# Placing the gate buffers of an attention and feed-forward kernel 128 bytes further on in SBUF

## The chip, the cores and the metric

The kernel runs on one NeuronCore of a Trainium2 chip. The metric is the device time of one execution in microseconds (us), the median over several runs. PE is TensorE, the matrix engine; PEld is its weight load, which overlaps its matmuls; DVE, ACT and POOL are VectorE, ScalarE and GpSimd; SP issues the DMAs. SBUF is the on-chip memory with 128 partitions, and an address here always means the byte within each partition at which a buffer begins. PSUM is the memory into which PE writes.

## What is computed

A chunked attention with memory tokens, and behind it a feed-forward layer with a piecewise quadratic gate:

```python
# attention: 4 batches, 8 heads, 768 tokens, head_dim 64; chunks of 32 queries,
# each sees 8 memory keys, 16 keys to the left, its own 32, and 8 to the right
for c in range(nc):
    ...
    scores = scale * np.matmul(q_c, k_full.transpose(0, 1, 3, 2))
    scores = scores - np.max(scores, axis=-1, keepdims=True)
    a = np.exp(scores)
    a = a / (np.sum(a, axis=-1, keepdims=True) + 1e-09)
    out[:, :, c_start:c_end] = np.matmul(a, v_full)
# feed-forward: 3072 tokens, 512 -> 2048 -> 512
h = x @ w_in
g = np.where(pos, h, np.where(neg, 0.0, (h + beta) ** 2 / (4.0 * beta)))   # beta 1, pos: h >= 1, neg: h <= -1
return (g @ w_out).astype(np.float32)
```

## The kernel before

**Tiling.** The 3072 tokens are six blocks of 512. In each block the attention output x (512 features as four slices of 128, times 512 tokens) is made in two halves and kept as two fp32r tiles, a high part `xth` and a remainder `xtl`. The feed-forward layer goes over 16 slices of 128 hidden features (`fc`). One step is one block and one slice, so there are 96 steps.

**A step on PE** has two groups of 12 matmuls.

- `pe_hidden` (line 406) makes the hidden values of the slice in a PSUM bank `ps_h`: four matmuls of the high weights with `xth`, four of the low weights with `xth`, four of the high weights with `xtl`. The stationary operand, the one that a weight load brings in, is a 128x128 piece of a weight tile `wr`; the moving operand is 512 tokens of x.
- `pe_out` (line 441), two steps later (`LAG`), multiplies the gated values with the slice of the second weight matrix into four PSUM banks `ps_o`: eight matmuls with `gh`, the high part of the gate, and four with `gl`, its remainder. Here the gate is the stationary operand (`gh[:, ts]`, 128 of its 512 columns, so 512 bytes per partition), and the moving operand is 512 columns of a weight tile `wr`.

Each matmul has a weight load of its own, and the load of the next matmul runs beside the present one.

**Between the groups** `gating` (line 415) has ACT read `ps_h` into `gw` and `gt` and square `gw`; `gate_sum` (line 425) has DVE combine them into `gw`; `gate_high` (line 430) has ACT round `gw` to `gh`; `gate_low` (line 436) has DVE write `gl` as the difference. So `gw`, `gt`, `gh` and `gl` are the gates' buffers: two each of `gw` and `gt`, three each of `gh` and `gl`, 2,048 bytes each in a partition.

**Order.** The program is written out in full, with no loop at run time, and each engine keeps the order in which it is written. The first two blocks follow a table (`FIRST`, lines 32 to 50) that interleaves DMA loads, decoding of the weights on ACT and DVE (`decode`, line 148), attention and steps; in it some steps are split into halves of 256 tokens (`early_step`, line 452). From step 32 on, the loop at line 573 puts attention for later blocks between the steps.

**Where buffers lie.** Four pools take SBUF from low addresses to high: `const` (weights), `xpool` (x), `apool` (attention, `f`, output), `gpool` (the gates). The compiled program gives these addresses:

| buffers | first address | spacing | address mod 512 |
|---|---|---|---|
| weights `w`, `wr`, 16 tiles | 1,664 | 8,192 | 128 |
| `xth`, `xtl`, two each | 132,736 | 8,192 | 128 |
| `pr`, `pt` | 177,792 | 4,096 | 128 |
| `f` (and `ob`), two | 194,560 | 4,096 | 0 |
| `gw`, `gt`, `gh`, `gl` | 202,752 | 2,048 | 0 |

The slices that PE reads are 512 bytes apart in the weights (as stationary operand) and in the gates, and 2,048 bytes apart in x and in the weights (as moving operand), so each slice has the remainder of its buffer.

Of the kernel before, what the change touches and what calls it, by code (L numbers as in the profile page):

```python
# [8 lines left out]
F32 = mybir.dt.float32  # L9
# [7 lines left out]
P = 128  # L17
# [51 lines left out]
def attn_ffn_kernel(ctx: ExitStack, tc: tile.TileContext, first_qk, first_v, qk, vw, w, out):  # L69
# [18 lines left out]
    gpool = ctx.enter_context(tc.tile_pool(name="gpool", bufs=2))  # L88
# [447 lines left out]
    early += [(load, blk, half) for blk, half in ((1, 1), (2, 0), (2, 1), (3, 0)) for load in (load_qk, load_v)]  # L536
    early = iter(early)

    warm = gpool.tile([P, DM], BF16, name="warm", tag="gw")
    dve.memset(warm, 0.0)  # L540
    keep_warm(8)
# [162 lines left out]
```

## Time and profile before

| | |
|---|---|
| time, median of 3 runs | 608.13 us (608.02 to 608.14) |
| span of the profiled execution, first to last instruction | 606.4 us |
| PE busy, instructions | 591.0 us (97%), 5496 |
| weight loads busy, instructions | 483.7 us (80%), 5496 |
| DVE busy | 325.6 us (54%) |
| ACT busy | 281.2 us (46%) |
| mean DMA rate | 91 GB/s |

For the profiled execution only its span is given; the 1.7 us between it and the median of the runs lie outside its first and last instruction. In the profile's lists "L63" is a helper that records every operation, so the groups are told apart by the names of their tiles: `ps_o<-wr,gh` is a matmul that reads `wr` and `gh` and writes `ps_o`. The time of a matmul in these lists is that of one alone, from its start to its modelled end; neighbours overlap, so the pace of PE is the distance from one start to the next.

### The profile page before, as it was taken

What the parts mean: (1) busy time and instruction counts of PE and PEld (TensorE: products, weight loads), DVE (VectorE), ACT (ScalarE), POOL (GpSimd) and SP (SyncE); (2) the same over time, 40 slices, a digit from 0 to 9 for tenths busy, and PEclk for the clock granted to TensorE, in tenths of its full rate; (3) what the DMA queues carried; (4) which work ended last, traced back from release to release, by engine and by line L of the source; (5) the groups of instructions that cost most, each with busy time, mean ns of one, the idle gap of its engine ahead of it and who ended that gap; (6) DMA issues with size and microseconds to landing.
All of it is one profiled execution on the core that took longest, in us unless ns stands there. A gap on an engine that the chain in (4) does not pass through costs nothing.

```text
span 606.4 us, 12265 instructions
## 1 busy us (share of the span) xinstructions
PE 591.0 (97%) x5496; PEld 483.7 (80%) x5496; DVE 325.6 (54%) x466; ACT 281.2 (46%) x503; POOL 0.7 (0%) x6
## 2 busy tenths in 40 slices
PE   5889999999999999999999999999999999999996
PEld 2888888888888888888888888888888888888885
DVE  5999999987483224736424734623553632322222
ACT  2689764544444434344434434434433343533342
POOL 0000000000000000000000000000000000000000
PEclk8699999999999999999999999999999999999999
DMA  8999200433131004012201213101310000100001
GB/s 353 423 418 420 124 1 1 175 110 137 31 145 70 1 0 175 30 42 105 70 1 73 103 70 106 70 1 54 121 70 2 1 2 0 70 0 1 0 1 69
DMA packets 9845, 55.31 MB, mean 91 GB/s; under 512 B 1089, under 2 KB 1089, under 8 KB 5185
## 3 DMA queue, kind: packets, MB, share of 16 engines
q1 hardware_dynamic: 9792, 54.53, 23.2%
q8 instruction: 43, 0.70, 0.5%
q14 instruction: 10, 0.07, 0.0%
HBM read 48.23 MB, written 6.29 MB: 90 GB/s over the span
## 4 chain that ended last, share of the span: by engine, by line
PE 94%; DVE 3%; ACT 1%; DMA 1%; issue 0%; DVEq 0%; ACTq 0%
PE ps_o L63 44%; PE ps_h L63 44%; PE ps_x L63 3%; PE ps_s L63 3%; DVE f L63 1%; DMA qk<-in_first_qk_dram 1%; DVE pr L63 1%; DVE mx L63 0%; DVE den L63 0%; ACT w L63 0%; ACT gw L63 0%; DVE wr L63 0%; DVE xtl L63 0%; ACT pr L63 0%; ACT wr L63 0%
## 5 line engine op out<-in xcount | busy, mean ns | idle before, releaser
L63 PE MATMUL ps_o<-wr,gh 128*128 128x512 f32 x768 | 199.5, 396 | 0.0
L63 PE MATMUL ps_h<-xth,wr 128*128 128x512 f32 (+1 forms) x832 | 197.3, 379 | 0.0
L63 PEld LDWEIGHTS ps_h<-xth,wr 128*128 128x128 f32 x832 | 148.7, 189 | 31.9 <-DVE wr L63 0.5
L63 PEld LDWEIGHTS ps_o<-wr,gh 128*128 128x128 f32 x768 | 143.7, 188 | 32.5
L63 DVE SCALAR_TENSOR_TENSOR gw<-gw,gt 128x512 f32<-128x512 f32 (+1 forms) x104 | 67.2, 648 | 170.0 <-ACT gw L63 169.5
L63 ACT ACTIVATE gw<-ps_h 128x512 f32<-128x512 f32 (+1 forms) x104 | 58.7, 564 | 167.8 <-PE ps_h L63 167.7
L63 PE MATMUL ps_o<-wr,gl 128*128 128x512 f32 x384 | 109.0, 394 | 0.0
L63 PE MATMUL ps_h<-xtl,wr 128*128 128x512 f32 (+1 forms) x416 | 105.2, 375 | 0.0
L63 DVE TENSOR_TENSOR gl<-gw,gh 128x512 fp32r<-128x512 f32 (+1 forms) x104 | 67.4, 649 | 67.4 <-ACT gh L63 67.3
L63 ACT CAST gh<-gw 128x512 fp32r<-128x512 f32 (+1 forms) x104 | 61.1, 590 | 68.7 <-DVE gw L63 68.7
L63 PEld LDWEIGHTS ps_h<-xtl,wr 128*128 128x128 f32 x416 | 75.3, 190 | 14.1
L63 PEld LDWEIGHTS ps_o<-wr,gl 128*128 128x128 f32 x384 | 72.5, 189 | 17.2
L63 ACT ACTIVATE gw<-gw 128x512 f32<-128x512 f32 (+1 forms) x104 | 62.5, 601 | 0.0
L63 ACT ACTIVATE gt<-ps_h 128x512 f32<-128x512 f32 (+1 forms) x104 | 58.2, 559 | 0.0
L63 DVE STREAM_TRANSPOSE pt<-pr 32x512 f32<-32x512 f32 (+1 forms) x60 | 41.2, 698 | 1.3
L63 DVE SCALAR_TENSOR_TENSOR f<-w,f 128x1024 uint32<-128x1024 uint32 x32 | 38.9, 1220 | 0.4
L63 PEld LDWEIGHTS ps_x<-pt,v 64*64 64x64 f32 x1536 | 25.2, 142 | 5.5 <-issue 3.5
L63 ACT ACTIVATE pr<-pr 128x1024 f32<-128x1024 f32 (+1 forms) x14 | 13.1, 937 | 35.5 <-DVE pr L63 35.4
L63 PE MATMUL ps_x<-pt,v 64*64 64x32 f32 x1536 | 26.7, 226 | 1.6 <-ACT pt L63 1.6
L63 ACT CAST xth<-ps_x 128x512 fp32r<-128x512 f32 x24 | 13.1, 590 | 21.6 <-PE ps_x L63 21.5
L63 PEld LDWEIGHTS ps_s<-qk 64*32 64x32 f32 x1536 | 16.7, 110 | 6.4 <-issue 3.2
L63 ACT CAST wr<-f 128x1024 fp32r<-128x1024 f32 x16 | 16.8, 1050 | 9.3 <-DVE f L63 9.3
(27 smaller groups left out, 182.1 us busy)
## 6 DMA issues: line engine op xcount, KB each, us to landing
w<-in_w_dram SPq DMA_DIRECT2D x16, 1024.0 KB, 19.8
qk<-in_qk_dram SPq DMA_DIRECT2D x10, 1536.0 KB, 6.7
v<-in_vw_dram SPq DMA_DIRECT2D x10, 1024.0 KB, 5.1
out_dram<-ob SPq DMA_DIRECT2D x24, 256.0 KB, 2.0
qk<-in_first_qk_dram SPq DMA_DIRECT2D x4, 768.0 KB, 8.8
v<-in_first_v_dram SPq DMA_DIRECT2D x4, 512.0 KB, 12.8
```

What stands on the lines that cost most here:

```text
L63: return self.tc.keep_in_program_order(getattr(self.engine, name)(*args, **kwargs))
```

## The change

One line is added ahead of the first tile of `gpool`. It takes a tile of 32 fp32 values, 128 bytes in each partition, that nothing reads or writes.

```diff
     early = iter(early)
 
+    gpool.tile([P, 32], F32, name="offset", bufs=1)
     warm = gpool.tile([P, DM], BF16, name="warm", tag="gw")
     dve.memset(warm, 0.0)
     keep_warm(8)
```

In the compiled program the gates' buffers (and `warm`, a bf16 tile that shares the first `gw` buffer and feeds eight matmuls at the start) begin at 202,880 in place of 202,752, and each of them lies 128 bytes further on; their address mod 512 is 128 in place of 0. No other buffer moves. Every engine has the same instructions with the same shapes in the same order as before; only the running numbers in the names of tiles and the line numbers behind line 538 differ by one.

## The prediction

> **What bounds the kernel now.** I read the page first: the busy shares, the clock and the chain that ended last.
>
> ```profile
> PE 591.0 (97%) x5496; PEld 483.7 (80%) x5496; DVE 325.6 (54%) x466; ACT 281.2 (46%) x503; POOL 0.7 (0%) x6
> ...
> PEclk8699999999999999999999999999999999999999
> ...
> PE 94%; DVE 3%; ACT 1%; DMA 1%; issue 0%; DVEq 0%; ACTq 0%
> ```
>
> PE is the bound, at full granted clock (9 in the row PEclk) after the first slices, and waits for almost nothing. Its time is therefore the number of matmuls times their pace. The groups with their shapes kept apart give the number:
>
> ```profile
> L63 PE MATMUL ps_o<-wr,gh 128*128 128x512 f32 x768 | 199.5, 396 | 0.0
> L63 PE MATMUL ps_h<-xth,wr 128*128 128x512 f32 x704 | 178.3, 395 | 0.0
> L63 PEld LDWEIGHTS ps_h<-xth,wr 128*128 128x128 f32 x832 | 148.7, 189 | 31.9 <-DVE wr L63 0.5 <-issue 0.2
> L63 PEld LDWEIGHTS ps_o<-wr,gh 128*128 128x128 f32 x768 | 143.7, 188 | 32.5
> ...
> L63 PE MATMUL ps_h<-xtl,wr 128*128 128x512 f32 x352 | 94.7, 391 | 0.0
> ```
>
> With half as many for `gl` that is 1152 matmuls of `ps_o` and 1056 of `ps_h` at 512 columns. Read alone, a matmul or a load takes the same time in both groups (395 and 396, 189 and 188 ns). The pace does not show here; it shows in the starts. Here is the timeline of PE over one step late in the run, when no attention work is left:
>
> ```profile
> 562.70 2.01 PE L63 MATMUL ps_h<-xth,wr 128*128 128x512 f32 x8
> 564.54 1.08 PE L63 MATMUL ps_h<-xtl,wr 128*128 128x512 f32 x4
> 565.45 2.03 PE L63 MATMUL ps_o<-wr,gh 128*128 128x512 f32 x8
> 567.32 1.09 PE L63 MATMUL ps_o<-wr,gl 128*128 128x512 f32 x4
> 568.25 0.40 PE L63 MATMUL ps_h<-xth,wr 128*128 128x512 f32 x1
> ```
>
> The step takes 568.25 - 562.70 = 5.55 us. `ps_o` has 2.80 us of it, 233 ns per matmul. `ps_h` has 2.75, but not evenly: the eight with `xth` run at 1.84 / 8 = 230 ns, the four with `xtl` at 0.91 / 4 = 227.5. The same twelve `ps_h` matmuls can do better, as the timeline shows at a place where they follow a different piece of work (a half step of `ps_o` after matmuls of 256 columns):
>
> ```profile
> 148.11 1.98 PE L63 MATMUL ps_h<-xth,wr 128*128 128x512 f32 x8
> 149.92 1.08 PE L63 MATMUL ps_h<-xtl,wr 128*128 128x512 f32 x4
> 150.83 0.40 PE L63 MATMUL ps_o<-wr,gh 128*128 128x512 f32 x1
> ```
>
> That is 2.72 us for twelve, 226.7 ns each, with `xth` at 226 as well. So `ps_h` has a settled pace of 226.7 ns and usually starts behind `ps_o` at a worse one that lasts for up to eight matmuls. Whether `ps_o` ever settles is seen at the end of the run, where three steps' groups of it stand in a row:
>
> ```profile
> 593.22 2.03 PE L63 MATMUL ps_o<-wr,gh 128*128 128x512 f32 x8
> 595.09 1.08 PE L63 MATMUL ps_o<-wr,gl 128*128 128x512 f32 x4
> 596.01 2.02 PE L63 MATMUL ps_o<-wr,gh 128*128 128x512 f32 x8
> 597.87 1.10 PE L63 MATMUL ps_o<-wr,gl 128*128 128x512 f32 x4
> 598.80 0.62 PE L63 MATMUL ps_o<-wr,gh 128*128 128x512 f32 x2
> 599.26 0.39 PE L63 MATMUL ps_o<-wr,gl 128*128 128x512 f32 x1
> 599.49 0.64 PE L63 MATMUL ps_o<-wr,gh 128*128 128x512 f32 x2
> 599.97 0.40 PE L63 MATMUL ps_o<-wr,gl 128*128 128x512 f32 x1
> ```
>
> It does not: 593.22 to 598.80 is 5.58 us for 24, 232.5 ns each, and the last four of them (597.87 to 598.80) still have 232.5. In this last stretch the other engines are nearly idle, as their timelines say:
>
> ```profile
> 596.44 0.69 DVE L63 TENSOR_TENSOR gl<-gw,gh 128x512 fp32r<-128x512 f32 x1 [0.69 <-ACT gh L63]
> ...
> 600.40 0.69 DVE L63 COPY ob<-ps_o 128x512 f32<-128x512 f32 x1 [3.27 <-PE ps_o L63]
> ...
> 601.12 0.59 ACT L63 COPY ob<-ps_o 128x512 f32<-128x512 f32 x1 [4.72 <-DVE ob L63]
> ```
>
> From 597.13 to 600.40 neither DVE nor ACT runs an instruction, and `ps_o` is as slow as ever. So contention with DVE or ACT is not what costs the 6 ns.
>
> **The change part by part.** It removes, adds and reorders no instruction, adds no wait, and moves no DMA. All that is new is where the gates lie: at 128 mod 512, as weights and x do.
>
> *ACT and DVE on the gates.* Rows of the same size whose buffer (`pr`) already lies at 128 mod 512 bound this:
>
> ```profile
> L63 DVE TENSOR_TENSOR gl<-gw,gh 128x512 fp32r<-128x512 f32 x88 | 60.8, 691 | 66.4 <-ACT gh L63 66.4
> ...
> L63 ACT ACTIVATE gw<-gw 128x512 f32<-128x512 f32 x88 | 55.7, 634 | 0.0
> ...
> L63 DVE TENSOR_TENSOR pr<-pr,rin 128x512 f32<-128x512 f32 x4 | 2.8, 692 | 0.1
> ...
> L63 ACT ACTIVATE pr<-pr 128x512 f32<-128x512 f32 x4 | 2.5, 624 | 8.1 <-DVE pr L63 8.1
> ```
>
> 692 against 691 and 624 against 634 ns: I take zero. The cover is that a gate is used two steps, about 11 us, after its `ps_h`; only in the first 205 us is there little of it.
>
> *The weight loads of gates.* This is the term. What differs between a load during `ps_h` and one during `ps_o` is the buffer it reads: `wr` at 128 mod 512, as the moving operand, or a gate at 0 mod 512, which is 384 away from it. The other differences are excluded by rows above. Output banks and the repeated moving operand: at the end the order is by output, so that one bank is written three times running with the moving operand alternating, and the five matmuls from 598.80 to 599.97 (1.17 us, 234 ns each) are no faster. Waits: most of these loads wait for nothing. So I expect `ps_o` to run at the settled pace of `ps_h`, and `ps_h` to lose its slow start, since it would follow a settled group. A group of `ps_o` then goes from 2.80 to 2.72 us (0.08 less), one of `ps_h` from 2.75 to 2.72 (0.03 less). The number of groups by stage, from the table by stages of the matmuls on one tile (the number behind x), first `ps_o` in three stages and then `ps_h` in the last:
>
> ```profile
> 0.00:107.00 107.00, 36.00 (x144) 0.92 0.60 247
> 107.00:205.00 98.00, 46.19 (x185) 1.00 0.28 103
> 205.00:602.00 397.00, 202.72 (x824) 1.00 0.12 45
> ```
>
> ```profile
> 205.00:602.00 397.00, 194.04 (x792) 1.00 0.12 45
> ```
>
> From 205 us on: 824 / 12 = 69 groups by 0.08 and 66 by 0.03 are 5.5 + 2.0 = 7.5 us. Of this I leave 0.3 for groups that follow small attention matmuls and may restart unsettled: the loop has two of those per half block, 12 for three blocks, and 0.03 for each is the unsettled part of a `ps_h` group. From 107 to 205: 15.4 by 0.08 and half of the remaining 22 groups of `ps_h` by 0.03, 1.2 + 0.3 = 1.5 us. Before 107: 12 by 0.08 and 11 by 0.03, 1.3 us. How much of the early terms reaches the end depends on DVE, which the table by stages shows for all engines (columns: PE, PEld, DVE, ACT):
>
> ```profile
> 62.00:107.00 45.00, 45.00 (x314) 36.35 (x312) 44.48 (x55) 28.06 (x44) 0.00 (x0) 1.00 0.08 30
> 107.00:145.00 38.00, 37.98 (x566) 33.02 (x566) 30.75 (x48) 19.47 (x45) 0.00 (x0) 1.00 0.41 150
> 145.00:205.00 60.00, 60.00 (x625) 49.34 (x625) 32.12 (x48) 25.40 (x48) 0.00 (x0) 1.00 0.20 73
> 205.00:595.00 390.00, 390.00 (x3124) 317.23 (x3123) 160.48 (x231) 163.18 (x292) 0.00 (x0) 1.00 0.13 46
> ```
>
> ```profile
> PEld ps_h L63 <- DVE wr L63: 0.5, 1, 0.5
> ```
>
> That wait, at 107 us, is PE arriving before DVE has decoded a weight tile, and DVE was busy 44.48 of the 45 us before it. A faster PE only waits longer there, so of the first 1.3 us I count nothing (at most 0.5, DVE's idle time). From 107 to 205 DVE still has 63 of 98 us, and chains through it end close to their use; I count 0.9 of 1.5. After 205 DVE and ACT are busy 41% and 42%, and all of it counts.
>
> Sum: 7.5 - 0.3 + 0.9 + 0 = 8.1 us. It is made on the span of 606.4, which becomes 598.3; the runs' median lies 1.7 above that span, and I keep that distance: **600.0 us**. Between the ends of its terms (early stages 0 to 2.0, late stage 6.7 to 7.5) and some tenths for rounded starts, this case alone runs from 598.4 to 602.
>
> [...] The trace shows two paces for two places of the loaded operand, 226.7 and 232.5 ns. [...]
>
> **The rivals.**
>
> *No effect: the place mod 512 is not the cause.* The gates differ from weights and x also in being at the top of SBUF, above 202,752, and in being written by ACT and DVE shortly before. If either makes their loads slow, 128 bytes change nothing: 608.1. For it: no two buffers in this trace differ in the remainder alone. Against it: the loads of `ps_h` come from weight tiles all the way from 1,664 to 132,735 and their means do not part (189 ns), so height alone costs little, and at 598 us the gates are long written. [...] Chance 0.19.
>
> *Half of it.* `ps_o` improves to what `ps_h` has now, 2.75 us a group, and neither settles, because changing from one group to the other disturbs the pace: 84 groups after 107 us by 0.05 are 4.2 us, so 604; between 602 and 606.9. For it: `ps_h` needs up to eight matmuls to settle. Against: at 148 us it settles at once. Chance 0.14.
>
> *Slower.* The two streams now start at the same place within 512 bytes in all matmuls, and if they meet at the same part of the memory, `ps_o` may stay at the worst pace it touches: 599.49 to 599.97 is 0.48 us for two, 240 ns each. Then the 185 + 824 = 1009 matmuls of `ps_o` after 107 us lose 240 - 233.3 = 6.7 ns each, 6.8 us: 615. It decides when the pace of `ps_o` passes 233.3. Against it: `ps_h` has just this relation and is the faster one. Chance 0.06, with any other loss.
>
> **How the numbers follow.** The forecast case has 0.61, half of it 0.14, no effect 0.19, slower 0.06. A measurement of this kernel can tell about 0.2%, 1.2 us, from no change, so faster is 0.61 + 0.14 = 0.75, same 0.19, slower 0.06. Without the case of no effect 0.25 would be left out, so the range reaches to it: 598.4 to 608.2.
>
> **What would show it.** Right: in late steps the distance between groups of `ps_h` falls from 5.55 to about 5.44 us, `ps_o` and `ps_h` both at 2.72; the run of `ps_o` at the end at 226 to 227 ns; the wait of the weight load for DVE's `wr` near 107 us longer by up to a microsecond. Wrong: `ps_o` still at 232 to 233 ns (the cause is not the remainder), or both groups at 2.75 (half), or an unchanged pace of PE with new waits after 205 us (another engine binds).

## The result, and the profile after

The changed kernel takes 600.09 us (median of 4 runs, 599.91 to 601.07) where the kernel before takes 608.11 (608.02 to 608.14, 4 runs): a ratio of 0.987, 95% interval 0.9858 to 0.9883. The profiled execution has a span of 598.3 us, 8.1 less than the 606.4 of before.

From the page of the changed kernel, the busy shares, the granted clock and the chain that ended last, by engine and by line:

```profile
PE 582.7 (97%) x5496; PEld 483.5 (81%) x5496; DVE 325.6 (54%) x466; ACT 280.3 (47%) x503; POOL 0.7 (0%) x6
...
PEclk9999999999999999999999999999999999999999
...
PE 82%; DVE 15%; issue 2%; DMA 1%; ACT 0%; DVEq 0%; ACTq 0%
PE ps_o L63 38%; PE ps_h L63 38%; DVE f L63 6%; PE ps_x L63 3%; DVE wr L63 2%; PE ps_s L63 2%; DVE gw L63 1%; DVE gl L63 1%; DVE pr L63 1%; DVE den L63 1%; DMA qk<-in_first_qk_dram 1%; DVE pt L63 1%; DVE mx L63 1%; DVE xtl L63 0%; DVE rin L63 0%
```

The page counts the same 5496 matmuls and weight loads and the same 466 DVE instructions; PE is busy 8.3 us less, DVE as before and ACT 0.9 us less. DVE's share of the last chain has gone from 3% to 15%: the early part of the run now hangs on the decoding of weights. The row PEclk differs from that of before in its first two slices (9 and 9, where it was 8 and 6). The gain does not come from that: the same `ps_h` matmul starts at 51.56 us before and at 51.54 after, and runs of the kernel before with a mean clock of 0.998 take 608.1 to 608.5 us, while runs of the changed kernel with 0.986 take 599.9 and 600.1.

The timeline of PE over a late step (`ps_h` of 12, `ps_o` of 12, and the next `ps_h`):

```profile
566.35 1.98 PE L63 MATMUL ps_h<-xth,wr 128*128 128x512 f32 x8
568.16 1.07 PE L63 MATMUL ps_h<-xtl,wr 128*128 128x512 f32 x4
569.07 1.98 PE L63 MATMUL ps_o<-wr,gh 128*128 128x512 f32 x8
570.88 1.07 PE L63 MATMUL ps_o<-wr,gl 128*128 128x512 f32 x4
571.78 1.98 PE L63 MATMUL ps_h<-xth,wr 128*128 128x512 f32 x8
```

The step takes 571.78 - 566.35 = 5.43 us in place of 5.55. Both groups take 2.72 or 2.71 us, 226 to 227 ns per matmul, from their first matmul on. And the groups of `ps_o` in a row at the end:

```profile
588.11 1.98 PE L63 MATMUL ps_o<-wr,gh 128*128 128x512 f32 x8
589.92 1.07 PE L63 MATMUL ps_o<-wr,gl 128*128 128x512 f32 x4
590.83 0.61 PE L63 MATMUL ps_o<-wr,gh 128*128 128x512 f32 x2
```

2.72 us for 12, 226.7 ns each, where it was 232.5.

Where the gain arises is seen from the starts of the same matmuls in both traces. Three places on PE's timeline, first before, then after: the `ps_h` group of the last weight slice of block 0, the first one behind the scores that follow, and the one at 206 us.

```profile
98.20 0.62 PE L63 MATMUL ps_h<-xth,wr 128*128 128x512 f32 x2
...
113.31 0.96 PE L63 MATMUL ps_h<-xth,wr 128*128 128x512 f32 x3
...
206.66 1.55 PE L63 MATMUL ps_h<-xth,wr 128*128 128x512 f32 x6
```

```profile
97.33 0.62 PE L63 MATMUL ps_h<-xth,wr 128*128 128x512 f32 x2
...
107.14 1.20 PE L63 MATMUL ps_h<-xth,wr 128*128 128x512 f32 x4 [1.09 <-DVE wr L63]
...
113.31 0.97 PE L63 MATMUL ps_h<-xth,wr 128*128 128x512 f32 x3
...
205.75 1.52 PE L63 MATMUL ps_h<-xth,wr 128*128 128x512 f32 x6
```

At 98 us PE is 0.87 us ahead, at 113 us nothing is left of it, and at 206 us it is 0.91 ahead. In between lies the wait for a decoded weight tile, which has grown from 0.5 to 1.5 us, as the list of waits after the change says (the first row is the weight load's wait, the second the matmul's behind it):

```profile
PEld ps_h L63 <- DVE wr L63: 1.5, 1, 1.5
...
PE ps_h L63 <- DVE wr L63: 1.1, 1, 1.1
```

From 206 us to the end the lead grows from 0.91 to 8.1 us, 7.2 us.

### The profile page after: what moved, and what is told of

It is laid out like the page before. It is cut to its first block, busy times and chain, and to the rows that moved or that the text cites. A ratio compares the mean times of both kernels' runs of the same rounds, so it can differ in the third digit from the quotient of the medians.

```text
span 598.3 us, 12265 instructions
## 1 busy us (share of the span) xinstructions
PE 582.7 (97%) x5496; PEld 483.5 (81%) x5496; DVE 325.6 (54%) x466; ACT 280.3 (47%) x503; POOL 0.7 (0%) x6
## 4 chain that ended last, share of the span: by engine, by line
PE 82%; DVE 15%; issue 2%; DMA 1%; ACT 0%; DVEq 0%; ACTq 0%
PE ps_o L63 38%; PE ps_h L63 38%; DVE f L63 6%; PE ps_x L63 3%; DVE wr L63 2%; PE ps_s L63 2%; DVE gw L63 1%; DVE gl L63 1%; DVE pr L63 1%; DVE den L63 1%; DMA qk<-in_first_qk_dram 1%; DVE pt L63 1%; DVE mx L63 1%; DVE xtl L63 0%; DVE rin L63 0%
## 5 line engine op out<-in xcount | busy, mean ns | idle before, releaser
L63 PE MATMUL ps_o<-wr,gh 128*128 128x512 f32 x768 | 194.7, 390 | 0.0
L63 PE MATMUL ps_o<-wr,gl 128*128 128x512 f32 x384 | 106.9, 389 | 0.0
```

The costliest lines, as they stand in the source:

```text
L63: return self.tc.keep_in_program_order(getattr(self.engine, name)(*args, **kwargs))
```

## The experiments

Theory A: what counts is the distance between the start of the loaded slice and the start of the moving operand, by its remainder. Theory B: the loaded slice's own place counts, 128 mod 512 being good and 0 bad. Theory C: any move of the gates does it.

**The gates moved by 512 bytes.**

```diff
-    gpool.tile([P, 32], F32, name="offset", bufs=1)
+    gpool.tile([P, 128], F32, name="offset", bufs=1)
```

> The unused tile ahead of the gates has 512 bytes in place of 128, so the gates lie 512 bytes further on than in the kernel before, again at 0 mod 512 (weights and x stay at 128). Theory A (the distance mod 512 between the loaded slice and the moving operand decides; 0 is good, 384 is bad): as before, 608.1 us, ps_o at 232.5 ns and 2.80 us per group. Theory B (the own place of the loaded slice mod 512 decides, 128 is good and 0 bad): also 608.1. Theory C (any move of the gates, or a tile in front of them, does it): 600.1 us, ps_o at 226.7 ns.

Measured: 608.08 us, ratio to before 0.9998 (0.9988 to 1.0008). PE's timeline late in this run, one line per group's first part:

```profile
568.37 2.01 PE L63 MATMUL ps_h<-xth,wr 128*128 128x512 f32 x8
...
571.13 2.03 PE L63 MATMUL ps_o<-wr,gh 128*128 128x512 f32 x8
...
573.93 2.01 PE L63 MATMUL ps_h<-xth,wr 128*128 128x512 f32 x8
```

2.76 and 2.80 us, as before. Theory C has fallen: a tile in front of the gates, and gates further up, change nothing by themselves.

**Everything at 0 mod 512.** The changed kernel, with weights, x, attention buffers and gates all 384 bytes further on:

```diff
+    const.tile([P, 96], F32, name="offset_w", bufs=1)
     ident = const.tile([P, P], F32, name="ident")
```

> The changed kernel with another unused tile of 384 bytes ahead of everything, so that weights, x and gates all begin at 0 mod 512. Theory A (distance): the distance is 0 everywhere, so 600.1 us and 226.7 ns in both groups. Theory B (own place, 0 is bad): now all loads are at the bad place, so both groups run at about 232.5 ns: 2208 matmuls by 5.8 ns above the settled pace are 12.8 us, less the early part that DVE hides, so 610 to 612 us.

Measured: 600.00 us, ratio 0.9866 (0.9849 to 0.9882). PE's timeline late in this run:

```profile
566.15 1.98 PE L63 MATMUL ps_h<-xth,wr 128*128 128x512 f32 x8
...
568.87 1.98 PE L63 MATMUL ps_o<-wr,gh 128*128 128x512 f32 x8
...
571.59 1.98 PE L63 MATMUL ps_h<-xth,wr 128*128 128x512 f32 x8
```

Both groups take 2.72 us with the gates back at 0 mod 512. Theory B has fallen: the place that is slow beside weights at 128 is as good as any beside weights at 0.

**x away from the weights.** The kernel before, with the 128 bytes ahead of x, so that gates and weights agree and x does not:

```diff
+    xpool.tile([P, 32], F32, name="offset_x", bufs=1)
     ident = const.tile([P, P], F32, name="ident")
```

> The kernel before with the 128 unused bytes ahead of x: x lies at 256 mod 512, the gates (which come behind it) at 128, and the weights stay at 128. The gates then match the weights, but the weights loaded in ps_h are at 384 mod 512 from x. Theory A (distance): the bad pace moves from ps_o to ps_h: ps_h at 232.5 ns, 2.79 us per group, ps_o with a slow start that settles, 2.75 us per group, so about 606 to 609 us. Theory B (own place; weights and gates are both at 128): 600.1 us and 226.7 ns in both.

Measured: 606.15 us, ratio 0.9967 (0.9954 to 0.998). PE's timeline late in this run:

```profile
566.49 2.02 PE L63 MATMUL ps_h<-xth,wr 128*128 128x512 f32 x8
568.35 1.10 PE L63 MATMUL ps_h<-xtl,wr 128*128 128x512 f32 x4
569.28 1.99 PE L63 MATMUL ps_o<-wr,gh 128*128 128x512 f32 x8
571.11 1.07 PE L63 MATMUL ps_o<-wr,gl 128*128 128x512 f32 x4
572.02 2.02 PE L63 MATMUL ps_h<-xth,wr 128*128 128x512 f32 x8
```

The two groups have changed roles: `ps_h` takes 2.79 us, 232.5 ns each and with `xtl` as slow as with `xth`, while `ps_o` takes 2.74 and ends at 0.91 / 4 = 227.5 for its last four. So it is the relation of the two operands that makes a group slow, whichever group it is.

**Only `gh` and `gl` moved.** The kernel before, with the 128 bytes between `gt` and `gh`:

```diff
+            gw, gt = gpool.tile([P, TB], F32, name="gw", tag="gw"), gpool.tile([P, TB], F32, name="gt")
+            if both.setdefault("offset", name) == name:
+                gpool.tile([P, 32], F32, name="offset", bufs=1)
             tiles = (
-                gpool.tile([P, TB], F32, name="gw", tag="gw"),
-                gpool.tile([P, TB], F32, name="gt"),
+                gw,
+                gt,
```

> The kernel before with the unused 128 bytes between gt and gh, so that only gh and gl, which PE loads, lie at 128 mod 512, and gw and gt, which only ACT and DVE use, stay at 0. If PE's loads are the cause: 600.1 us. If the place of what ACT and DVE read and write has a part in it: between 600.1 and 608.1.

Measured: 600.00 us, ratio 0.9866 (0.9851 to 0.9881). PE's timeline late in this run:

```profile
568.85 1.98 PE L63 MATMUL ps_o<-wr,gh 128*128 128x512 f32 x8
...
571.57 1.98 PE L63 MATMUL ps_h<-xth,wr 128*128 128x512 f32 x8
```

`ps_o` takes 2.72 us, as in the changed kernel. The whole gain comes from the two tiles that PE loads; where ACT and DVE have `gw` and `gt` has no part in it.

**The matmuls alone.** A kernel with none of the attention and feed-forward work: 36 matmuls with 36 loads in a row for each pair of places. One more row of the first pair runs ahead of them and is not counted.

```python
for m in (0, 128):                    # moving operand, 512 columns, fp32r
    for at in range(0, 512, 32):      # loaded operand
        group(("f", at), ("f", m))
for at in range(0, 512, 32):          # bf16
    group(("h", at), ("h", 0))
```

> Only matmuls of 512 columns, none of the kernel's work: 36 in a row for each of 16 places of the loaded tile (0, 32, ... 480 mod 512), first with the moving tile at 0 mod 512, then all again with it at 128, in fp32r; then the 16 places in bf16 with the moving tile at 0. Theory A (distance): the pace as a function of the place shifts by 128 bytes between the first and the second 16; 226.7 ns at distance 0, and about 232.5 ns at distance 384, so at place 384 in the first series and at place 0 in the second. Theory B (own place): the two series are the same, and place 0 is slow in both.

Some rows of PE's timeline, where the number behind `sta` is the place of the loaded tile and that behind `mov` the place of the moving one; the pace is the distance to the next row's start, over 36:

```profile
24.61 8.55 PE L63 MATMUL ps<-mov0f,sta32f 128*128 128x512 f32 x36
33.00 8.56 PE L63 MATMUL ps<-mov0f,sta64f 128*128 128x512 f32 x36
...
83.22 8.33 PE L63 MATMUL ps<-mov0f,sta256f 128*128 128x512 f32 x36
91.39 8.55 PE L63 MATMUL ps<-mov0f,sta288f 128*128 128x512 f32 x36
...
116.60 8.53 PE L63 MATMUL ps<-mov0f,sta384f 128*128 128x512 f32 x36
124.97 8.55 PE L63 MATMUL ps<-mov0f,sta416f 128*128 128x512 f32 x36
...
150.00 8.56 PE L63 MATMUL ps<-mov128f,sta0f 128*128 128x512 f32 x36
158.39 8.56 PE L63 MATMUL ps<-mov128f,sta32f 128*128 128x512 f32 x36
...
183.44 8.33 PE L63 MATMUL ps<-mov128f,sta128f 128*128 128x512 f32 x36
191.61 8.55 PE L63 MATMUL ps<-mov128f,sta160f 128*128 128x512 f32 x36
...
283.61 7.94 PE L63 MATMUL ps<-mov0h,sta0h 128*128 128x512 bf16 x35
291.38 7.93 PE L63 MATMUL ps<-mov0h,sta32h 128*128 128x512 bf16 x35
```

With the moving tile at 0, place 256 gives 8.17 / 36 = 226.9 ns, place 32 gives 233.1, place 384 gives 232.5. With the moving tile at 128, place 0 gives 233.1 and place 128 gives 226.9. ACT, DVE and POOL run nothing between 9.5 us, when the copies of the operands are done, and 408 us, so no row shown has another engine at work. All 32 pairs, as the mean of the last 28 distances between starts in each row of the trace:

| distance, mod 256 | 0 | 32 | 64 | 96 | 128 | 160 | 192 | 224 |
|---|---|---|---|---|---|---|---|---|
| ns per matmul, fp32r | 226.7 | 233.3 to 233.4 | 233.3 to 233.4 | 234.3 | 232.4 to 233.4 | 233.3 to 233.5 | 228.9 | 233.3 to 233.4 |

The second series is the first one shifted by 128 bytes, as theory A has it, but for one row: at a distance of 128, three rows have 232.4 and the first row with the moving tile at 128 has 233.4. So one distance can have two paces. What theory A had not said is the period: places 256 bytes apart give the same, so the remainder mod 256 is enough. In bf16 all 16 places give 7.76 to 7.78 us for 36 (7.77 from 283.61 to 291.38; the trace lacks the record of one matmul in most of these rows), 215.8 ns: there the place of the loaded tile has no effect. In bf16 the moving tile was at 0 alone.

**Three more places of the gates**, each the changed kernel with another size of the unused tile: 96, 80 and 56 fp32 values for 384, 320 and 224 bytes.

```diff
-    gpool.tile([P, 32], F32, name="offset", bufs=1)
+    gpool.tile([P, 96], F32, name="offset", bufs=1)
```

> The unused tile ahead of the gates has 384 bytes, so the gates lie at 384 mod 512, a distance of 256 from weights and x. If the distance counts mod 256 (as the row of matmuls alone shows, 226.7 ns at distances 0 and 256 alike): 600.1 us and 226.7 ns in both groups. If in the kernel it counts mod 512, as the change says: about 608 us, ps_o at 232 to 234 ns.

Measured: 600.08 us, ratio 0.9868 (0.9853 to 0.9882), the same as with an equal place mod 512. The distance counts mod 256 in the kernel too.

> The unused tile has 320 bytes, a distance of 192 from the weights. If the pace by distance of the matmuls alone holds in the kernel (228.9 ns at 192): ps_o 2.75 us per group, 0.053 less than before on 84 groups behind the wait at 107 us, 4.5 us, and for ps_h, whose start is open, 0 to 0.03 on 77 groups: 601.5 to 604.5 us. If only an equal place helps and any other is like before: 608.

Measured: 602.08 us, ratio 0.9901 (0.9884 to 0.9917). PE's timeline late in this run:

```profile
568.11 1.98 PE L63 MATMUL ps_h<-xth,wr 128*128 128x512 f32 x8
...
570.83 2.00 PE L63 MATMUL ps_o<-wr,gh 128*128 128x512 f32 x8
...
573.58 1.98 PE L63 MATMUL ps_h<-xth,wr 128*128 128x512 f32 x8
```

`ps_o` takes 2.75 us, 229 ns each, as the matmuls alone have it at 192, and `ps_h` settles at once (2.72).

> The unused tile has 224 bytes, a distance of 96 from the weights, the worst place for the matmuls alone (234.3 ns against 232.4 at the place of before). If that holds in the kernel: 1009 matmuls of ps_o by 1.9 ns, 1.9 us more than before, about 610 (609 to 611, the start of ps_h being open). If it does not: 608.

Measured: 607.99 us, ratio 0.9992 (0.9983 to 1.0001): not the loss that was expected. PE's timeline late in this run:

```profile
567.95 1.99 PE L63 MATMUL ps_h<-xth,wr 128*128 128x512 f32 x8
...
570.68 2.03 PE L63 MATMUL ps_o<-wr,gh 128*128 128x512 f32 x8
...
573.49 1.99 PE L63 MATMUL ps_h<-xth,wr 128*128 128x512 f32 x8
```

`ps_o` takes 2.81 us, 234 ns each, so its pace is the worst one, as expected. But `ps_h` takes 2.73 in place of 2.75: behind this `ps_o` it settles sooner. The step is 5.54 us where it was 5.55. From 206 us on, the mean distance between starts is 1.1 ns longer for `ps_o` than in the kernel before and 1.6 ns shorter for `ps_h`, and the two cancel. How long `ps_h` needs to settle differs with the group ahead of it (2.75 us behind a `ps_o` at a distance of 128, 2.73 at 96, 2.72 at 192), and the pace in a long row does not give it.

**Finer steps, and 256 columns.** Again matmuls alone, with one moving and one loaded tile and slices of them:

```python
for s in (0, 4, 8, 12, 16, 20, 24, 28, 228, 232, 236, 240, 244, 248, 252):
    group(s, 0, 512)      # place of the loaded slice, of the moving one, columns
for s in range(0, 256, 32):
    group(s, 64, 512)
for s in range(0, 512, 64):
    group(s, 0, 256)
```

> Matmuls alone again, 36 in a row for each pair, fp32r, none of the kernel's work: the moving tile at 0 mod 512 and the loaded one 4 to 28 and 228 to 252 bytes on in steps of 4; then the moving operand at 64 with the loaded one at 0 to 224 in steps of 32; then 256 columns in place of 512, the loaded one at 0 to 448 in steps of 64. If the distance mod 256 decides: with the moving operand at 64 the pace is 226.7 at place 64 alone. Whether a distance of less than 32 bytes already costs is open: 226.7 if the start within 32 bytes does not matter, up to 233.3 if it does. No pace below 226.7 is expected. At 256 columns: 120 ns at distances 0 and 256, more elsewhere if the cost is one per load, by up to 6 ns.

Measured, as the mean of the last 28 distances between starts in each row of 36 (a row at 0 and 0 ahead of them is not counted):

| | |
|---|---|
| 512 columns, moving at 0, distance 0, 4, 8, 12, 16, 20, 24, 28 | 226.7, 232.4, 230.7, 230.0, 233.3, 233.4, 231.2, 235.0 ns |
| the same, distance 228, 232, 236, 240, 244, 248, 252 | 230.6, 231.1, 231.7, 228.3, 233.3, 233.3, 226.7 ns |
| 512 columns, moving at 64, loaded at 0, 32, 64, 96, 128, 160, 192, 224 | 228.8, 233.3, 226.7, 233.4, 233.3, 234.3, 232.4, 233.3 ns |
| 256 columns, moving at 0, loaded at 0, 64, 128, 192, 256, 320, 384, 448 | 120.0, 117.8, 118.8, 117.8, 120.0, 113.4, 118.6, 117.8 ns |

With the moving operand at 64, the place with 226.7 ns is 64, so the distance decides once more. Four bytes already cost 5.7 ns one way and nothing the other way. At 256 columns the expectation was wrong: there the equal places (0 and 256, 120.0 ns) are the slowest of the eight, and 320 (113.4) the fastest. Each place has one row here, in one execution.

## Why the prediction was right

**The term.** The prediction gave `ps_o` the settled pace of `ps_h`, 226.7 ns, and took the slow start of `ps_h` for a thing that `ps_o` leaves behind. Both came true: `ps_h` takes 2.72 us per group in place of 2.75, and `ps_o` 2.71 to 2.72 in place of 2.80. `x_at_256` shows the second half from the other side, since there it is `ps_o` that starts slowly behind a slow `ps_h` and settles.

**The stages.** Before 107 us it counted nothing, since DVE was busy nearly all the time (44.48 of the 45 us) and PE would only wait longer: PE came 0.87 us early and gave all of it back.

From 107 to 205 it counted 0.9 of 1.5, and 0.91 was measured, but here the reason was wrong and the agreement is luck. The prediction took off 0.6 for chains through DVE. From 113 to 206 us PE waits for nothing in either trace, so nothing was lost that way; the pace itself gained less. In this stretch nine groups of `ps_o` follow matmuls of 256 columns or of the attention. Two of the nine, with the work behind each, first before, then after:

```profile
142.51 1.08 PE L63 MATMUL ps_o<-wr,gh 128*128 128x512 f32 x4
...
145.29 1.11 PE L63 MATMUL ps_h<-xth,wr 128*128 128x256 f32 x8
...
146.72 1.08 PE L63 MATMUL ps_o<-wr,gh 128*128 128x512 f32 x4
...
148.11 1.98 PE L63 MATMUL ps_h<-xth,wr 128*128 128x512 f32 x8
```

```profile
142.38 1.09 PE L63 MATMUL ps_o<-wr,gh 128*128 128x512 f32 x4
...
145.13 1.12 PE L63 MATMUL ps_h<-xth,wr 128*128 128x256 f32 x8
...
146.56 1.09 PE L63 MATMUL ps_o<-wr,gh 128*128 128x512 f32 x4
...
147.95 1.98 PE L63 MATMUL ps_h<-xth,wr 128*128 128x512 f32 x8
```

The group of 12 goes from 2.78 to 2.75 us, not to 2.72, and the half group of six stays at 1.39: with the gates at the good place too, a group behind such matmuls starts slowly and settles only after five or six.

Behind 205 us it counted 7.5 - 0.3: measured 7.2. The 0.3 was left out for 12 groups of `ps_h` behind attention matmuls, and by the starts in both traces these 12 gain nothing indeed. Of the whole, `ps_o` gave 5.1 us where 5.5 was counted, and `ps_h` 2.0 where 2.0 - 0.3 was: the rounded gains per group, 0.08 and 0.03, were a little too large and a little too small, and the two errors cancel.

**The exclusions.** That DVE and ACT do not cause the slow pace rested on 3 us at the end of the run in which they were idle; the matmuls alone have the same pace (232.5 ns at place 384) with no other engine at work, and `gh_gl_only` has the whole gain (600.00 us) without moving what only DVE and ACT use. The rival of no effect named the height of the buffers and their writers. In the changed kernel the gates still lie at the top and ACT and DVE still write them, and the slow pace is gone (226.7 ns where it was 232.5), so neither makes it. The prediction's argument against height was weaker than that: its row of 189 ns is one mean over the loads from all weight tiles and cannot show that their means do not part. That 128 bytes mod 512 are not a good place of themselves is shown by `all_at_0`, where the gates are at 0 and the gain is there (600.00 us). Settling in half, the second rival, did not occur in the late steps: where the two groups follow each other, the pace is 226 to 227 ns from the first matmul of a group on.

**What it did not know.** "The same place within 512 bytes" is more than is needed: the same place within 256 is enough (226.9 ns at place 256 with the moving tile at 0, and 600.08 us in `gates_384`). The slower rival, an equal place that is the worst, is wrong for these matmuls, which have 226.7 ns there; at 256 columns the two equal places, with 120.0 ns, were the slowest of the eight tried.

**The two paces.** The trace before had 226.7 and 232.5 ns for two places of the loaded operand. The rows of matmuls alone show how far this goes: in bf16 they have 215.8 ns at every place, in fp32r 226.7 to 235.0 ns, changing with the place. No run here shows what makes the difference between the two formats.

**What stays open.** Why the pace depends on the distance was not settled, nor why it goes in cycles away from the good places (at a distance of 128 the distances between starts repeat after seven matmuls, from 228 to 241 ns, as for `ps_o` in the trace before from 593.22 to 601.35 us): the runs show where it happens, not what meets what. In all runs the matmul that runs beside a load and the one that uses it have their moving operands at the same place mod 512 within a group, so the runs do not tell which of the two the load has to match. The prediction spoke of settling without a cause for it, and still has none.

## What to carry to other kernels

Where PE is the bound and every fp32r matmul of 512 columns has its own weight load, try the loaded tiles and the moving ones at the same address mod 256 (226.7 ns per matmul here, 228.3 to 235.0 at the other distances but 252); an unused tile in front of a pool does it (128 bytes in each partition here), and it cost no time (608.08 us with the 512 bytes of `gates_512`, 608.1 without). Read the pace from the distance between starts, not from the time of one matmul (395 and 396 ns in the two groups before, whose settled paces were 226.7 and 232.5), and compare the groups of one kernel with each other: a group that runs slower than another with the same shapes is a hint. Do not carry this over to bf16, where the place had no effect (215.8 ns at all of 16), or to 256 columns, where the equal places were the slowest of the eight tried (120.0 ns, 113.4 at the fastest), without measuring.

## What the runs showed of the hardware that was not expected

- fp32r matmuls of 512 columns with a load each settle at 226.7 ns when the two operands start at the same place mod 256, or the loaded one 4 bytes short of it, and run at 228.3 to 235.0 ns at the other distances that were tried.
- The same in bf16 run at 215.8 ns at all of 16 places.
- At 256 columns in fp32r the equal places (0 and 256) give 120.0 ns and the others less, 113.4 ns at 320; 64, which is 320 less 256, gives 117.8, so these rows do not show the period of 256 bytes. They do not rule it out either: with 512 columns one distance (128) was seen at two paces, 232.4 and 233.4 ns.
